# Weight decoding in a Performer and MLP kernel: a third raw buffer, and two pieces of w1 decoded later

## The chip, the cores and the metric

The kernel runs on one core of one Trainium2 chip. The metric is device time in microseconds (us) of one execution, and the figure compared is the median of several executions. The engines are named as the profile names them: PE is TensorE's matmul, PEld its weight load, DVE VectorE, ACT ScalarE, POOL GpSimd and SP SyncE, which issues the DMAs. Each engine takes its own instructions in the order of its queue. The DMAs of this kernel stand nearly all in SyncE's queue, one behind the other.

## The reference

Everything is computed from 64-bit inputs; the kernel reads their words and decodes the weights to 32-bit floats by itself.

```python
def phi(x):                       # random features, omega is 128 x 64
    h = x @ omega.T - sum(x * x) / 2
    return exp(h - max(h)) / sqrt(m)
q_p, k_p = phi(q * scale), phi(k * scale)      # batch 8, heads 8, seq 576, head_dim 64
num = q_p @ (k_p.T @ v)
den = q_p @ sum(k_p)
x = num / (den + 1e-6)                         # heads side by side: 8 x 576 x 512
u = x + (x.T @ U @ V).T                        # mixing along the sequence, rank 32
out = u + relu(u @ w_ch1) @ w_ch2              # w_ch1 512 x 2048, w_ch2 2048 x 512
```

## The kernel before

**Stages.** The first stage is attention: 16 units (pairs of heads), in rounds of nine steps, one step for each tile of 128 positions. A round works on the keys of one unit and the queries of another. In one step TensorE multiplies by the features (`project`, L525 to L527, tile `p_p`), VectorE takes the maximum (L533), ScalarE the exponential (`exp`, L540, tile `e`), and TensorE uses `e` for the keys' sums (L437) or transposes it for the queries (L463). In between runs the mixing along the sequence (`mixing`), which writes rows of `u` to DRAM. The second stage is the MLP over 36 tiles of 128 tokens, in nine chunks: the first of six tiles, seven of four, the last of two.

**The MLP.** The first chunk (`whole_pass`) goes over 16 blocks `f` of 128 hidden features. A block consists of the first product for block f + 1 (`whole1`, L845, 24 matmuls into `p_p`: a group of 512 tokens and one of 256), a relu on ScalarE (L853) and VectorE (L854) for each group, and the second product of block f (`second`, L917, 18 matmuls). All float32 operands are split in a high and a low part, and each product has three passes. The chunks of four tiles take the first product with seven products in place of eight (`products`, L893), pair of blocks by pair of blocks, eight pairs `p` to a chunk; their weight operands `wx` are made once and then read back from DRAM, seven loads a pair (L760).

**Decoding.** `decoding` (L103) is a generator over 35 jobs: one for U, two for V, 16 pieces of w1 (512 columns of 128 rows each) and 16 tiles of w2. A job's 64-bit words come into a tile `raw`, of which there are RB = 2. Then ScalarE takes the magnitude (`mag`, L120), VectorE works on it in a fixed order, one instruction at each step of the generator, and GpSimd adds the low word's share (L164). An early job has five VectorE steps (L139, L140, L143, L146, L147). A late one (number `lean` and up) has three, and a second ScalarE pass makes its low word's share (`low`, L123). The last VectorE step is the last reading of `raw`; behind it the generator asks for the load of job i + RB (L158). The add and what follows are put off into the next job's steps: for w1 a ScalarE copy into `w1f` (L185), for w2 a ScalarE copy into the high part (L177) and a subtraction on GpSimd for the low part (L178). The tiles `mag` and the tag `de` have two buffers each.

**What sets the order.** The code is written in the order in which the work is wanted, and `keep_in_program_order` fixes the order of marked instructions on their engine: the loads of raw weights, VectorE's decoding steps, ScalarE's copies of decoded weights, and nearly all of the MLP. The rest, L120, L123, L164 and L178 among it, is ordered when the program is built, by a simulated timeline. In attention `advance` (L260) takes a decoding step in two of three steps, until `left` = 6 + 5 * EARLY = 66 are used; EARLY = 12 jobs, U, V, six pieces of w1, two tiles of w2 and one piece more. In the MLP's first chunk `each(f, i)` (L997) is called four times a block and takes 1, 2, 1 and 2 decoding steps. From there on, pieces of w1 and tiles of w2 alternate (L198). Block f uses w1's columns for block f + 2 (`Halves`) and w2's tile f.

**Chunks to come.** `Chunk.fetch` (L779) loads a quarter of the next chunk's `u` into a tile `uraw`, of which the pool `up` has three buffers, and `turn` (L784) transposes it on VectorE into `uT`. In the first chunk the fetches come in blocks 6, 7, 8 and 10 and the turns in blocks 9 to 12; in a middle chunk three fetches come at pairs 0, 1 and 2 and the fourth behind the first turn, in pair 5.

Of the kernel before, what the change touches and what calls it, by code (L numbers as in the profile page):

```python
# [9 lines left out]
F32 = mybir.dt.float32  # L10
# [4 lines left out]
ALU = mybir.AluOpType  # L15
# [14 lines left out]
def performer_mlp_kernel(ctx: ExitStack, tc, q, k, v, omega, U, V, w1, w2, out):  # L30
# [7 lines left out]
    nc = tc.nc  # L38
# [3 lines left out]
    DM, DF = w1.shape  # L42
    P = 128
# [7 lines left out]
    NC = DM // P  # L51
    NF = DF // P
# [5 lines left out]
    def f32(ap):  # L58
        return ap.bitcast(F32)

    def words(ap):
        return ap.bitcast(U32)
# [6 lines left out]
    CT, TOK = 4, 4 * P  # L69
# [9 lines left out]
    AHEAD = 2  # L79
    LEAD = AHEAD  # L80
    w1f = const.tile([P, NC, DF], F32, name="w1f")
    w2s = {f: [const.tile([P, DM], F32R, name=f"w2{a}{f}") for a in "hl"] for f in range(AHEAD)}
# [15 lines left out]


    PIECE = 512  # L100
    RB = 2

    def decoding(jobs, late, lean):  # L103

# [7 lines left out]
        def fetch(i):  # L112
            if i < len(jobs):
                raws[i] = dec.tile([P, PIECE, 2], U32, name="raw", bufs=RB)[:, : jobs[i][1], :]
                jobs[i][0](raws[i])
# [8 lines left out]

        for i in range(RB):
            fetch(i)
# [4 lines left out]
        for i, job in enumerate(jobs):  # L131
# [19 lines left out]
            for j, slot in enumerate(slots):  # L151
# [5 lines left out]
                if j == len(slots) - 1:  # L157
                    fetch(i + RB)  # L158
                yield
# [8 lines left out]
            rest.pop(0)()  # L168
            yield

    def weights(src, parts):
        def load(raw):
            tc.keep_in_program_order(nc.sync.dma_start(out=raw.rearrange("p n w -> p (n w)"), in_=words(src)))

        return (
            load, PIECE,
            lambda w: tc.keep_in_program_order(nc.scalar.copy(out=parts()[0], in_=w)),  # L177
            lambda w: nc.gpsimd.tensor_tensor(out=parts()[1], in0=w, in1=f32(parts()[0]), op=ALU.subtract),  # L178
        )

    def w1_job(i):
        f, c = divmod(i, NC)
        fs = slice(f * PIECE, (f + 1) * PIECE)
        load = weights(w1[c * P : (c + 1) * P, fs], None)[0]
        return load, PIECE, lambda w: tc.keep_in_program_order(nc.scalar.copy(out=w1f[:, c, fs], in_=w))  # L185


    N1, FIRST = DF // PIECE * NC, 6

    def w2_job(f):  # L190
        return weights(w2[f * P : (f + 1) * P, :], lambda: w2s[f])

    def weight_jobs():
        for i in range(FIRST):
            yield w1_job(i)
        for f in range(AHEAD):
            yield w2_job(f)
        for i in range(max(N1 - FIRST, NF - AHEAD)):  # L198
            if FIRST + i < N1:
                yield w1_job(FIRST + i)  # L200
            if AHEAD + i < NF:
                yield w2_job(AHEAD + i)

# [54 lines left out]
    def advance(gen, n=1, late=False):  # L260
        for _ in range(n):
            if late or left[0] > 0:
                left[0] -= 1
                if next(gen, gen) is gen:
                    return False
        return True
# [116 lines left out]
    class Part:  # L383
# [20 lines left out]
        def low(self):  # L404
            self.xl.append(wk.tile([P, G * P], F32R, name="xl", bufs=4))
            nc.gpsimd.tensor_tensor(out=self.xl[-1], in0=self.turned, in1=f32(self.xh[-1]), op=ALU.subtract)  # L406
# [196 lines left out]
    }  # L603
    steps = {}
    decoder = decoding([u_job(), *v_jobs(), *weight_jobs()], 6, EARLY)
    mixers = []
    x = None
# [80 lines left out]
    up = ctx.enter_context(tc.tile_pool(name="up", reuse_waits="tile", bufs=2))  # L688
# [82 lines left out]
    class Chunk:  # L771
# [6 lines left out]

        def fetch(self):  # L779
            j = len(self.raws)  # L780
            self.raws[j] = up.tile([P, TOK], F32, name="uraw", bufs=3)[:, : self.n * P]
            fetch(self.c, {j: self.raws[j]})

        def turn(self):  # L784
# [73 lines left out]
        def products(self, w, between):  # L858

            bank = lambda n, b: ps.tile([P, HT], F32, name="p_s", tag=n, bufs=b)  # L860
            X, Y, Z, W = bank("p_p", 2), bank("p_p", 2), bank("p_m", 1), bank("p_kv", 1)
            near = dec.tile([P, 4, HT], F32, name="near", tag="raw", bufs=RB)
            far = dec.tile([P, 2, HT], F32, name="far", tag="de", bufs=2)
# [72 lines left out]
    def take(steps, n=None):  # L936
        while n is None or n > 0:
            if next(steps, steps) is steps:
                return
            n = None if n is None else n - 1  # L940
# [32 lines left out]
    rp = ctx.enter_context(tc.tile_pool(name="rp", side="right", reuse_waits="tile", bufs=2))  # L973
# [21 lines left out]
    pairs, nxt = Weights(0), Chunk(1)  # L995

    def each(f, i):  # L997
        advance(decoder, 1 + i % 2, True)
        if i == 0 and f in (6, 7, 8, 10):
            nxt.fetch()  # L1000
        if 9 <= f < 13 and i == 0:
            nxt.turn()
        if f == 13 and i == 0:
            nxt.prepare()
        if 13 <= f < 15 and i == 1:
            nxt.add()
        if f == 14:
            pairs.add()
            one.residual((4, 5, 0, 1)[i])
        if f == NF - 1:  # L1010
            while advance(decoder, 1, True):
                pass
            while len(pairs.ops) < 5:
                pairs.add()
            while len(nxt.ops) < 3:
                nxt.add()

    steps = whole_pass(one, g, each)
    for c in range(1, NCH - 1):
        now, nxt = nxt, Chunk(c + 1)  # L1020
        short = nxt.n < CT
        for p in range(NH):
            new = None
            if p + 1 < NH or not short:
                new = Weights(p + 1) if c == 1 and p + 1 < NH else Again((p + 1) % NH)
            if p < 3:
                nxt.fetch()
            if p == NH - 1:
                if not short:
                    nxt.add()  # L1030

            def between(i):
                take(steps, 4 - i % 2)
                if p == 6 and i == 6 and not short:
                    nxt.prepare()
                if p > 4 and i % 4 == 0 and nxt.turned < NC:
                    nxt.turn()
                    if nxt.turned == 1:
                        nxt.fetch()
                if len(now.ops) < 7:  # L1040
                    now.add()
                if len(pairs.ops) < 7:
                    pairs.add()
                if new and len(pairs.ops) == 7:
                    new.add()
                    if i == 6:
                        while len(new.ops) < 7:
                            new.add()
                if p == NH - 1 and i < 6:
                    if not short:  # L1050
                        nxt.add()
                    elif i in (0, 2):
                        nxt.short(nxt.uT[:, i : i + 2, :HT], nc.vector)
                    elif i in (1, 3):
                        ws[i // 2] = Halves(i // 2)

            g = now.products(pairs, between)
            take(steps)
            pairs = new
            if p == NH - 1:  # L1060
                for t in range(CT):
                    now.residual(t)
            steps = now.second([p, p + NH], [[x] for x in g], p == 0, p == NH - 1)
# [39 lines left out]
```

## Time and profile before

| | us |
|---|---|
| median of 3 executions | 1155.08 (1154.62 to 1155.59) |
| profiled execution, its own time | 1160.14 |
| its span, first to last instruction | 1158.4 |
| mean granted TensorE clock | 0.975 |

| stage (us of the span) | length | PE busy | DVE busy | ACT busy | POOL busy |
|---|---|---|---|---|---|
| 100 to 200, attention | 100 | 93.27 | 91.46 | 78.23 | 55.44 |
| 200 to 300, attention | 100 | 96.27 | 86.31 | 82.68 | 54.18 |
| 300 to 400, its end and the MLP's begin | 100 | 92.02 | 69.65 | 56.18 | 37.82 |
| 525 to 600, the first middle chunk | 75 | 73.40 | 47.58 | 29.50 | 35.67 |
| 600 to 1095, the other middle chunks | 495 | 495.00 | 233.24 | 111.83 | 26.55 |

A row of a view of waits names who waited, for whom, the time in all, how often and the longest single wait. A row of the chain of waits has a start, a length and what the end of the kernel hung on in that time. A row of the timeline has start, length, engine, line, operation, tiles and count. A row of instruction groups has line, engine, operation, tiles, shapes and count, then busy time and mean ns of one, then the engine's idle time before them. A matmul's end is modelled, so that TensorE's pace is best read from starts.

### The profile page before, as it was taken

To read this page: it belongs to the slowest core of one execution; us is meant where nothing else is said; L and a number is where in the kernel's file an instruction comes from. 1 tells how busy PE (TensorE), PEld (TensorE's weight loads), DVE (VectorE), ACT (ScalarE), POOL (GpSimd) and SP (SyncE) were. 2 spreads that over 40 slices of the span, in tenths; PEclk is the share of its full clock that TensorE was granted. 3 is DMA by queue.
4 is the path that set the end of the run, shared out by engine and by line. 5 is a ranking of instruction groups with operands and counts; after the bars stand their busy time and mean duration, and the time that the engine had idled before them with its cause. 6 is when DMAs were issued, how large, how long until landed. Compare 5 with 4: busy or idle time off the path is not lost.

```text
span 1158.4 us, 20643 instructions
## 1 busy us (share of the span) xinstructions
PE 1107.9 (96%) x7105; PEld 995.1 (86%) x7105; DVE 676.6 (58%) x1475; ACT 500.7 (43%) x1403; POOL 342.6 (30%) x353
## 2 busy tenths in 40 slices
PE   8988989989988989989999999999999999999998
PEld 7988978989967867778988988988999998898887
DVE  4777989977994555455573463463463553553421
ACT  5877868879864554334331132131231221221222
POOL 3435636636315555555420010010100100100133
PEclk9988989999997999989999999999999999999999
DMA  7687676675252345067578687687687687686510
GB/s 130 132 155 137 119 171 135 128 165 103 85 101 82 109 128 128 19 201 236 191 217 232 182 229 220 182 228 220 182 234 212 183 254 193 183 249 187 170 56 19
DMA packets 344360, 187.93 MB, mean 162 GB/s; under 512 B 275872, under 2 KB 275872, under 8 KB 344256
## 3 DMA queue, kind: packets, MB, share of 16 engines
q1 hardware_dynamic: 344192, 186.55, 61.5%
q8 instruction: 57, 0.93, 0.3%
q14 instruction: 47, 0.39, 0.1%
q0 software_dynamic: 64, 0.07, 0.0%
HBM read 152.99 MB, written 33.55 MB: 161 GB/s over the span
## 4 chain that ended last, share of the span: by engine, by line
PE 67%; DVE 8%; DMA 5%; issue 2%; ACT 2%; POOL 1%; SPq 0%; DVEq 0%; ACTq 0%; POOLq 0%
PE p_s L893 23%; PE p_n L917 15%; PE p_q L917 14%; DMA raw<-in_moe_w_ch_dram 4%; PE p_p L845 4%; PE p_n L483 2%; PE p_kv L437 2%; DVE mag L140 2%; PE p_q L463 1%; PE p_p L525 1%; DVE mag L143 1%; PE p_p L526 1%; PE p_p L527 1%; PE py L322 1%; DVE nm L533 1%
## 5 line engine op out<-in xcount | busy, mean ns | idle before, releaser
L893 PEld LDWEIGHTS p_s<-ux,wx 128*128 128x128 f32 x2352 | 336.5, 191 | 43.4 <-ACT near L871 2.6
L893 PE MATMUL p_s<-ux,wx 128*128 128x256 f32 x2352 | 347.2, 284 | 6.1 <-DVE far L701 2.8
L917 PE MATMUL p_n<-w2h,g 128*128 128x512 f32 x576 | 196.6, 398 | 0.0
L917 PE MATMUL p_q<-w2h,g 128*128 128x512 f32 x512 | 191.3, 397 | 0.0
L540 ACT ACTIVATE e<-p_p,nm 128x128 f32<-128x128 f32 x576 | 167.1, 384 | 30.9 <-DVE nm L533 22.1
L406 POOL TENSOR_TENSOR xl<-xT,xh 128x384 fp32r<-128x384 f32 x96 | 100.9, 1067 | 145.4 <-ACT xh L402 107.5
L917 PEld LDWEIGHTS p_n<-w2h,g 128*128 128x128 f32 x576 | 110.0, 191 | 14.4
L814 POOL TENSOR_TENSOR us<-uT 128x512 f32<-128x512 f32 x14 | 19.2, 1368 | 341.1 <-DVE uT L787 341.1
L853 ACT ACTIVATE g<-far 128x256 fp32r<-128x256 f32 x112 | 46.8, 418 | 161.7 <-DVE far L701 161.7
L917 PE MATMUL p_n<-w2l,g 128*128 128x512 f32 x288 | 114.9, 399 | 0.0
L533 DVE TENSOR_REDUCE nm<-p_p 128x4 f32<-128x512 f32 x144 | 97.9, 680 | 28.2 <-PE p_p L527 18.9
L701 DVE TENSOR_TENSOR near<-p_s,near 128x256 f32<-128x256 f32 x168 | 70.4, 419 | 73.7 <-PE p_s L893 71.9
L845 PE MATMUL p_p<-ux,wx 128*128 128x256 f32 (+1 forms) x576 | 100.8, 331 | 11.8 <-DVE g L854 9.7
L845 PEld LDWEIGHTS p_p<-ux,wx 128*128 128x128 f32 x576 | 89.0, 196 | 26.4 <-DVE g L854 12.6
L698 POOL TENSOR_TENSOR wx<-w1f,wx 128x256 fp32r<-128x256 f32 x88 | 66.4, 771 | 129.1 <-ACT wx L697 129.1
L854 DVE SCALAR_TENSOR_TENSOR g<-p_s,g 128x256 fp32r<-128x256 f32 x56 | 23.8, 424 | 135.3 <-ACT g L853 135.3
L917 PEld LDWEIGHTS p_q<-w2h,g 128*128 128x128 f32 x512 | 93.4, 190 | 10.3
L917 PE MATMUL p_q<-w2l,g 128*128 128x512 f32 x256 | 101.5, 397 | 0.0
L853 ACT ACTIVATE g<-p_s 128x256 fp32r<-128x256 f32 x56 | 21.6, 385 | 184.8 <-PE p_s L893 184.6
L525 PE MATMUL p_p<-omh,xh 128*128 128x256 f32 x288 | 95.3, 331 | 0.6 <-ACT e L540 0.3
L854 DVE SCALAR_TENSOR_TENSOR g<-p_p,g 128x256 fp32r<-128x256 f32 (+1 forms) x48 | 24.5, 511 | 110.5 <-ACT g L853 110.5
L526 PE MATMUL p_p<-oml,xh 128*128 128x256 f32 x288 | 83.4, 290 | 0.0
(120 smaller groups left out, 1934.7 us busy)
## 6 DMA issues: line engine op xcount, KB each, us to landing
wx<-wx_dram SPq DMA_DIRECT2D x336, 256.0 KB, 3.0
raw<-in_moe_w_ch_dram SPq DMA_DIRECT2D x32, 512.0 KB, 4.1
wx_dram<-wx SPq DMA_DIRECT2D x56, 256.0 KB, 2.5
u_dram<-ut SPq DMA_DIRECT2D x36, 256.0 KB, 2.1
u<-u_dram SPq DMA_DIRECT2D x36, 256.0 KB, 4.4
out_dram<-u SPq DMA_DIRECT2D x36, 256.0 KB, 3.2
kt<-in_k_dram SPq DMA_DIRECT2D x120, 72.0 KB, 2.8
qt<-in_q_dram SPq DMA_DIRECT2D x120, 72.0 KB, 2.8
```

Of the source, the lines that this page charges most:

```text
L406: nc.gpsimd.tensor_tensor(out=self.xl[-1], in0=self.turned, in1=f32(self.xh[-1]), op=ALU.subtract)
L525: nc.tensor.matmul(o, part.xh[g][:, ts], oh, start=True, stop=False)
L526: nc.tensor.matmul(o, part.xh[g][:, ts], ol, start=False, stop=False)
L533: nc.vector.tensor_reduce(out=self.nm[:, :n], in_=self.pp[:, :n], axis=AX.X, op=ALU.max, negate=True)
L540: nc.scalar.activation(out=self.e[:, j, :], in_=self.pp[:, j, :], func=AF.Exp, bias=self.nm[:, j : j + 1])
L698: keep(rest.tensor_tensor(out=hl[:, 1], in0=x, in1=f32(hl[:, 0]), op=SUBTRACT))
L701: keep(nc.vector.tensor_tensor(out=out, in0=a, in1=b, op=op))
L845: nc.tensor.matmul(ph, l, r, start=(cc + i == 0), stop=(cc == NC - 1 and i == 2))
L853: keep(nc.scalar.activation(out=g[:, 0, ts], in_=x, func=AF.Relu))
L854: keep(nc.vector.scalar_tensor_tensor(out=g[:, 1, ts], in0=x, scalar=0.0, in1=f32(g[:, 0, ts]), op0=ALU.max, op1=ALU.subtract))
L893: tc.keep_in_program_order(nc.tensor.matmul(o, l, r, start=(i in (0, 1, 2, 5) and k + j == 0), stop=(k == 1 and j == 2), skip_group_check= ...
L917: tc.keep_in_program_order(nc.tensor.matmul(po, l, r, start=(begin and n + i == 0), stop=(end and n == len(fs) - 1 and i == 2)))
```

## The change

- RB, the number of `raw` buffers, goes from 2 to 3. The tile `near` of the seven products has the same tag and so three buffers too.
- The subtraction that makes w2's low parts stays on GpSimd for the first two tiles and goes to VectorE for the other 14. It is not marked to keep its place.
- FIRST, the pieces of w1 decoded early, goes from 6 to 4. With it EARLY becomes 10, the early steps 56, and the late jobs 25 of three steps. The late order begins with four pieces of w1 and one tile of w2 (the first of the pieces still as the last early job) and alternates from there.
- In the MLP's first chunk a block takes 2, 2, 2 and 1 decoding steps, seven in place of six.
- `uraw` moves from `up`, three buffers, to the pool `rp`, two buffers. In the first chunk the fetches come in blocks 6, 7, 9 and 10, and behind the turn of the same block; in a middle chunk two come at pairs 0 and 1 and the others behind the first and the second turn.

```diff
-    RB = 2
+    RB = 3
...
-    def weights(src, parts):
+    def weights(src, parts, low=nc.gpsimd.tensor_tensor):
...
-            lambda w: nc.gpsimd.tensor_tensor(out=parts()[1], in0=w, in1=f32(parts()[0]), op=ALU.subtract),
+            lambda w: low(out=parts()[1], in0=w, in1=f32(parts()[0]), op=ALU.subtract),
...
-    N1, FIRST = DF // PIECE * NC, 6
+    N1, FIRST = DF // PIECE * NC, 4
...
     def w2_job(f):
-        return weights(w2[f * P : (f + 1) * P, :], lambda: w2s[f])
+        low = nc.gpsimd if f < AHEAD else nc.vector
+        return weights(w2[f * P : (f + 1) * P, :], lambda: w2s[f], low.tensor_tensor)
...
-        for i in range(max(N1 - FIRST, NF - AHEAD)):
-            if FIRST + i < N1:
-                yield w1_job(FIRST + i)
-            if AHEAD + i < NF:
-                yield w2_job(AHEAD + i)
+        for i in range(FIRST, FIRST + 4):
+            yield w1_job(i)
+        yield w2_job(AHEAD)
+        for i in range(max(N1 - FIRST - 4, NF - AHEAD - 1)):
+            if FIRST + 4 + i < N1:
+                yield w1_job(FIRST + 4 + i)
+            if AHEAD + 1 + i < NF:
+                yield w2_job(AHEAD + 1 + i)
...
-            self.raws[j] = up.tile([P, TOK], F32, name="uraw", bufs=3)[:, : self.n * P]
+            self.raws[j] = rp.tile([P, TOK], F32, name="uraw", bufs=2)[:, : self.n * P]
...
     def each(f, i):
-        advance(decoder, 1 + i % 2, True)
-        if i == 0 and f in (6, 7, 8, 10):
-            nxt.fetch()
+        advance(decoder, 1 + (i < 3), True)
         if 9 <= f < 13 and i == 0:
             nxt.turn()
+        if i == 0 and f in (6, 7, 9, 10):
+            nxt.fetch()
...
-            if p < 3:
+            if p < 2:
                 nxt.fetch()
...
                     nxt.turn()
-                    if nxt.turned == 1:
+                    if nxt.turned < 3:
                         nxt.fetch()
```

## The prediction

> **What bounds the kernel now.** I read the page first, then the waits by engine, the chain of waits, and windows over the two stages that the change touches.
>
> ```profile
> span 1158.4 us, 20643 instructions
> ...
> PE 1107.9 (96%) x7105; PEld 995.1 (86%) x7105; DVE 676.6 (58%) x1475; ACT 500.7 (43%) x1403; POOL 342.6 (30%) x353
> ```
>
> TensorE bounds the whole, so only TensorE's gaps are worth anything. They lie in two stages: attention (up to about 350 us) and the first block of the MLP, which decodes the rest of the weights while it multiplies (about 365 to 475 us). For that second stage the waits are:
>
> ```profile
> POOL mag L164 <- DVE mag L143: 47.4, 23, 4.0
> ...
> ACT low L123 <- DMA raw<-in_moe_w_ch_dram: 25.8, 20, 2.4
> ACT w2h L177 <- POOL mag L164: 22.2, 11, 2.5
> PEld p_p L845 <- DVE g L854: 12.6, 8, 3.9
> PE p_p L845 <- DVE g L854: 9.7, 4, 3.5
> ```
>
> ScalarE waited 25.8 us, in 20 places, for the raw weights to land. It takes its instructions in order, so the relu (L853) behind L123 waited too, then VectorE's half of the relu (L854), and TensorE waited for that one. The chain of waits shows one turn of the loop, two pieces long:
>
> ```profile
> 388.33 4.16 DMA raw<-in_moe_w_ch_dram
> ...
> 392.51 0.02 ACT low L123
> ...
> 393.09 0.59 ACT g L853
> ...
> 393.70 0.69 DVE g L854
> ...
> 394.97 0.43 DVE mag L140
> ...
> 396.49 1.41 DVE mag L140
> ...
> 397.92 0.70 DVE mag L143
> ...
> 398.68 4.74 DMA raw<-in_moe_w_ch_dram
> ```
>
> L143 is a late piece's last reading of its raw buffer. With two buffers the load for the piece after the next can start only then, and its 4.2 to 4.7 us stand in the loop. A turn is 398.68 - 388.33 = 10.35 us and decodes two pieces. What it costs TensorE, from the windows of the first product (L845) and from the chain behind the last piece:
>
> ```profile
> 369.00:482.50 113.50, 54.50 (x289) 46.49 (x290) 0.98 0.39 105
> ...
> 482.62 4.17 PE p_p L845 x24
> ...
> 490.99 1.16 PE p_p L845 x5
> ```
>
> A block has 24 such products. 289 of them are 12 blocks in 113.5 us, 9.46 us each. Without decoding a block takes 490.99 - 482.62 = 8.37 us. The excess is 113.5 - 12 x 8.37 = **13.1 us**.
>
> In attention the same wait is rarer and longer:
>
> ```profile
> ACT mag L120 <- DMA raw<-in_moe_w_ch_dram: 11.5, 5, 3.8
> ...
> ACT low L123 <- DMA raw<-in_moe_w_ch_dram: 3.5, 1, 3.5
> ...
> PE p_q L463 <- ACT e L540: 12.4, 5, 3.7
> ```
>
> Its price I read from the length of rounds of nine steps. Here are the windows between the first L533 of each round (length; L533's busy time and count; granted clock; DMA share; GB/s):
>
> ```profile
> 65.80:88.70 22.90, 6.13 (x9) 0.85 0.84 157
> 88.70:113.00 24.30, 6.12 (x9) 0.86 0.75 148
> ...
> 133.30:158.00 24.70, 6.07 (x10) 0.88 0.66 148
> 158.00:177.70 19.70, 6.02 (x9) 0.98 0.73 161
> 177.70:198.00 20.30, 6.14 (x9) 1.00 0.70 140
> 198.00:218.90 20.90, 6.18 (x10) 1.00 0.59 122
> 218.90:241.00 22.10, 6.00 (x9) 0.99 0.69 154
> 241.00:258.90 17.90, 6.16 (x10) 0.91 0.69 152
> 258.90:276.60 17.70, 6.17 (x9) 1.00 0.66 122
> ```
>
> Three kinds are seen: rounds that decode without a long wait (19.7, 20.3, 20.9: mean 20.3), rounds with one (22.9, 24.3, 24.7, 22.1), and rounds after the last early piece (17.9, 17.7: mean 17.8).
>
> **The change, part by part.**
>
> *Third raw buffer, attention.* Each load now waits for the piece three before it, not two, so it is issued a whole piece earlier: five steps at two in three steps of attention, 7.5 steps or some 17 us at 20.3/9 us a step. Against that the longest wait was 3.8 us. No load should be late any more. The four rounds give back (22.9 + 24.3 + 24.7 + 22.1) - 4 x 20.3 = **12.8 us**. The waits on ScalarE, 15.0 us, bound it from above. From below I take 8, if the last round, which mixes two kinds, and one more give nothing.
>
> The granted clock of 0.85, 0.86 and 0.88 in those rounds is part of their length. The Trainium skill's "TensorE: Matmul & The Clock Gate" (What's actually happening) says that the array drops to half rate after an idle window of about 3.4 us and comes back after as long a busy one. The trace agrees: only the rounds with a wait are that low. By that rule one would add 0.15 x 22.9 + 0.14 x 24.3 + 0.12 x 24.7 = 9.8 us to the gain, as an estimate. I don't, because rounds are compared whole and the clock is in them already.
>
> *Third raw buffer, at the start.* The second piece of V is now loaded at once, not after the first job. Its four transfers stand in SyncE's queue ahead of the third set of values, for which TensorE already waits. The wait, and the same four transfers of the first piece:
>
> ```profile
> PE p_kv L437 <- DMA x<-in_v_dram: 1.7, 1, 1.7
> ...
> 29.09 1.89 SPq L236 DMA_DIRECT2D raw<-in_moe_V_dram  x4
> ```
>
> That costs **1.9 us** if nothing covers it; between 0 and 4, if the gap lowers the clock too.
>
> *Two pieces fewer in attention.* The early steps fall from 66 to 56. A round has six steps, and decoding costs a round 20.3 - 17.8 = 2.5 us, 0.42 us a step; ten steps are **4.2 us**. Between 2 (if the later rounds were shorter for another reason) and 6.
>
> *The same pieces in the MLP, and seven steps a block.* 25 late pieces of three steps take 75 steps, 10.7 blocks of seven; before, 23 pieces took 69, 11.5 blocks of six. A block so decodes 2.33 pieces, not 2. Each has two ScalarE passes over the raw tile (L120, L123) and one copy, three VectorE steps, a GpSimd add, and on SyncE one load of 512 KB that now waits for an older buffer. Cover is TensorE's 8.37 us a block:
>
> ```profile
> 365.00:475.00 110.00, 100.21 (x488) 82.51 (x487) 61.54 (x95) 56.36 (x111) 60.77 (x58) 0.99 0.41 111
> ...
> L178 POOL TENSOR_TENSOR w2l<-mag,w2h 128x512 fp32r<-128x512 f32 x16 | 21.1, 1317 | 4.1 <-ACT w2h L177 4.0
> ...
> L283 DVE TENSOR_TENSOR ml<-x,mh 128x512 fp32r<-128x512 f32 x9 | 6.8, 756 | 0.3 <-ACT mh L282 0.3
> ...
> L140 DVE TENSOR_SCALAR mag<-mag x23: 406/427/1402, 365.8 to 473.6; 128x512 uint32<-128x512 uint32 x23
> ```
>
> These are the block's stage (length, then busy time of PE, PEld, DVE, ACT and POOL), a low part on GpSimd, the same form on VectorE, and one decoding step (shortest, median and longest ns). Busy time for each 9.46 us block is 5.29 us on VectorE, 4.85 on ScalarE, 5.23 on GpSimd. Times 7/6 that is at most 6.2, 5.7 and 6.1.
>
> *Low parts of w2 on VectorE.* 1.17 of them a block leave GpSimd at 1.32 us each (6.1 becomes 4.6) and come to VectorE, where the same form (L283) takes 0.76: 6.2 + 0.9 = 7.1 us, still under 8.37. If the two engines meet it is dearer. L140 takes 0.43 alone and up to 1.40 beside GpSimd's add, 0.98 more; with that on every low part VectorE has 8.2 us a block, barely covered. The Trainium skill speaks against this edit: "Perfetto Trace Analysis" (Optimizing Scalar/DVE Operations) says that the two engines share an SBUF port, so that moving work between them might not help. L140's spread agrees. I count nothing for this move, so the sum is the same by the page.
>
> *What is late next in the block.* The load leaves the loop, since the piece it serves is two pieces, 7 us, further on, against 4.2 to 4.7 us of landing. Left in order are ScalarE's waits for GpSimd's add (22.2 us in 11), which have other work to fill them now, and a shorter lead: the first late w2 piece has its low part at step 15 and is multiplied after step 18; before it was step 6 against 15. I leave 3 us of the 13.1 for these: gain **10 us**, between 7 and 13.1.
>
> *Raw tiles of u in two buffers.* In each of six middle chunks SyncE now waits for a second transposition, with the next pair's weight loads queued behind:
>
> ```profile
> SPq L350 <- DVE uT L787: 17.8, 6, 3.0
> ...
> uraw<-u_dram SPq DMA_DIRECT2D x112, 64.0 KB, 3.9
> ...
> 655.49 0.70 DVE L787 STREAM_TRANSPOSE uT<-uraw 128x512 f32<-128x512 f32 x1
> ...
> 666.13 0.70 DVE L787 STREAM_TRANSPOSE uT<-uraw 128x512 f32<-128x512 f32 x1
> ```
>
> One such wait is 3.0 us. The tile loaded after the second turn (655.49) is transposed at 666.13, 9.9 us after its buffer is free; four issues (1.9 us for V's) and a landing (3.9) are 5.8 us. A weight load has about one pair of lead (10.6 us between the same turns of two pairs). Nothing is counted. The other order of fetch and turn in the first block, the larger decoding pool and its third `near` tile move no work.
>
> **Sum:** 12.8 - 1.9 + 4.2 + 10 = 25.1 us off. The profiled execution took 1160.14 us (span 1158.4), 5.1 above the median of 1155.08, and by the same sum would take 1135.0. The median becomes 1155.1 - 25.1 = **1130.0 us**.
>
> **The rivals.**
>
> *A: the block keeps its pace.* ScalarE's wait for GpSimd's add, already 22.2 us, takes the place of the wait for the load. Then 10 us are lost and the time is 1140. For it: both waits stand on the same in-order engine. Against: 25.8 us of the other go, and ScalarE has 5.7 us of work in 8.37. Chance 0.14.
>
> *B: attention keeps its late loads*, since SyncE reaches them late behind the query and key loads; the third buffer does not do there what it says. 12.8 us are lost: 1142.8. Against: a piece of lead is 17 us. Chance 0.07.
>
> *C, slower: VectorE becomes the bound in the block.* A low part waits in VectorE's order for ScalarE's high part, which waits for GpSimd's add. By the rows that is 2.0 us (22.2/11) and a copy of 0.6; with 0.76 and 0.98 it is 4.4 us for each piece, 5.1 a block. VectorE would have 6.2 + 5.1 = 11.3 us a block: eleven blocks of 11.3 and one of 8.37 are 132.7 us, 19.2 more than now. Against 15.1 from attention the time is 1159. It decides from 10.8 us a block, where a low part holds VectorE 3.9 us. Against: the next piece's steps can stand ahead of it. Chance 0.04.
>
> *D: SyncE's new wait delays the weight loads* of the middle chunks. From 7 us of wait on, each us costs six; 4 us over would eat the gain: 1154, no change. Against: 3.0 us. Chance 0.03.
>
> **How the numbers follow.** The forecast has 0.72. Its own range is the sum of the bounds: 8 - 4 + 2 + 7 = 13 at the least, 15 - 0 + 6 + 13.1 = 34 at the most; the low ends will hardly all meet, so I take 18 to 34, 1121 to 1137. To leave out no more than two in ten it takes in A and B: 1121 to 1143. What a measurement here can tell is 0.2%, 2.3 us. Faster are the forecast, A and B: 0.93; the same is D: 0.03; slower is C: 0.04.
>
> **What would show it.** Right: no wait of L120 or L123 for the raw load over 1 us; rounds of decoding attention near 20.3 us with the clock near 1.0, and the last early decoding step some 40 us sooner; blocks near 8.6 us between 365 and 475; the wait at the third values near 3.6 us. Wrong: blocks still over 9 us, with L177 behind L164 or VectorE's low part behind L177; or new waits at L893 in the middle chunks.

## The result and the profile after

The median after is 1128.73 us (1126.68 to 1130.28, four executions), against 1155.34 us before (1154.62 to 1157.26, four executions). The ratio is 0.9766, with an interval of 0.9745 to 0.9787: 26.6 us off, where 25.1 were forecast. The profiled execution took 1129.66 us of its own (before: 1160.14), with a mean granted clock of 0.983.

First the page's span and busy times, as they were shown of before:

```profile
span 1127.9 us, 20592 instructions
...
PE 1096.9 (97%) x7105; PEld 986.4 (87%) x7105; DVE 683.9 (61%) x1485; ACT 500.2 (44%) x1405; POOL 328.1 (29%) x339
```

TensorE has the same 7105 matmuls, and GpSimd has 14 instructions fewer, the low parts that went to VectorE. Lines behind the weights' part have moved by 5: L845 is now L850, L853 and L854 are L858 and L859, L893 is L898, L533 is L538, L350 is L355, L787 is L792. L120 to L178 stay.

To see where the time went, three stages are cut at two places that each kernel has: the start of the first matmul of the first product (L850 after, L845 before) and the start of the first one of the seven products (L898, L893). The places are the first starts in the views of those two lines, here after (shortest, median and longest ns, first and last start in us):

```profile
L850 PE MATMUL p_p<-ux,wx x576: 274/284/793, 328.8 to 1121.1; 128*128 128x256 f32 x128, 128*128 128x512 f32 x64
L898 PE MATMUL p_s<-ux,wx x2352: 274/283/580, 468.7 to 1072.2; 128*128 128x256 f32 x196
```

| kernel | attention and its end | blocks | rest | median | ratio to before, 95% interval |
|---|---|---|---|---|---|
| before | 350.6 | 148.7 | 659.2 | 1155.34 | |
| before_again, one execution | 351.9 | 144.4 | 658.7 | 1156.73 | |
| after | 328.8 | 139.9 | 659.2 | 1128.73 | 0.9766 (0.9745 to 0.9787) |
| after_again, one execution | 331.0 | 139.4 | 658.3 | 1130.54 | |
| two_buffers | 338.3 | 152.4 | 660.3 | 1151.61 | 0.9974 (0.9946 to 1.0001) |
| buffer_room | 335.8 | 135.8 | 658.3 | 1132.08 | 0.9783 (0.9734 to 0.9832) |
| pieces_only | 337.2 | 155.4 | 658.5 | 1156.18 | 1.0003 (0.9975 to 1.0031) |
| low_on_pool | 329.1 | 142.7 | 658.8 | 1132.12 | 0.9789 (0.9732 to 0.9847) |
| room_only | 350.6 | 146.1 | 661.1 | 1153.93 | 0.9996 (0.9974 to 1.0018) |
| late_fetch | 329.2 | 138.1 | 658.6 | 1127.67 | 0.9769 (0.9741 to 0.9796) |
| v_later | 330.3 | 137.0 | 660.4 | 1128.19 | 0.9767 (0.9730 to 0.9804) |
| five_pieces | 330.9 | 136.1 | 658.1 | 1125.70 | 0.9730 (0.9711 to 0.9748) |
| low_kept | 330.0 | 136.7 | 658.7 | 1124.76 | 0.9726 (0.9707 to 0.9746) |
| five_kept | 329.2 | 136.2 | 659.7 | 1126.09 | 0.9744 (0.9717 to 0.9771) |

The stages are of the one profiled execution, the medians of all. Between the two profiled executions of before the blocks differ by 4.3 us, though it is the same program, and attention by 1.3; a difference of that size in one row of the table proves nothing. Attention gave 21.7 us (20.9 between the second looks), the blocks 8.8 (4.9), the rest nothing.

**Attention after.** The windows between the first L538 of each round, from round 3 to round 10, here with all engines (length; busy time and count of PE, PEld, DVE, ACT and POOL; granted clock; DMA share; GB/s):

```profile
68.10:85.30 17.20, 16.50 (x145) 15.82 (x144) 16.84 (x43) 14.79 (x51) 9.65 (x9) 1.00 0.84 153
85.30:103.90 18.60, 18.20 (x155) 17.33 (x155) 18.23 (x46) 17.11 (x55) 12.40 (x11) 1.00 0.86 149
103.90:124.00 20.10, 20.01 (x164) 19.05 (x163) 19.25 (x44) 19.38 (x61) 15.58 (x14) 1.00 0.85 158
124.00:143.50 19.50, 18.45 (x147) 16.74 (x147) 19.42 (x48) 15.14 (x51) 8.06 (x7) 1.00 0.86 175
143.50:164.10 20.60, 19.36 (x155) 17.60 (x155) 19.58 (x47) 15.29 (x51) 9.26 (x8) 1.00 0.86 196
164.10:183.50 19.40, 18.16 (x147) 16.80 (x147) 19.22 (x45) 17.07 (x53) 14.53 (x12) 1.00 0.72 143
183.50:203.60 20.10, 20.10 (x165) 19.23 (x165) 15.85 (x40) 18.05 (x57) 13.52 (x13) 1.00 0.54 104
203.60:221.10 17.50, 17.50 (x153) 17.11 (x151) 16.52 (x42) 13.90 (x48) 5.91 (x6) 1.00 0.71 160
```

Rounds 3, 4, 6 and 10, which took 22.9, 24.3, 24.7 and 22.1, take 17.2, 18.6, 19.5 and 17.5. The clock is 1.00 in all eight. Before, rounds 3, 4 and 6 each held one stretch at half the clock, as narrower windows over that trace show (length, PE busy and count, granted clock, DMA share, GB/s):

```profile
70.00:76.90 6.90, 6.08 (x28) 0.51 0.73 117
97.30:104.20 6.90, 6.79 (x32) 0.51 0.84 136
152.00:158.80 6.80, 6.53 (x29) 0.50 0.53 135
```

At half the clock these 20.6 us cost 10.3. In ScalarE's waits from 60 to 245 us there is no raw tile any more; the longest row is the maximum of VectorE:

```profile
ACT e L545 <- DVE nm L538: 14.4, 23, 1.6
```

The last decoding step of the early kind (L147) starts at 180.3, before at 228.5, from the view of that line:

```profile
L147 DVE SCALAR_TENSOR_TENSOR de<-raw,de x10: 446/684/1439, 40.2 to 180.3; 128x512 f32<-128x512 uint32 x7, 128x288 f32<-128x288 uint32 x2, 128x320 f32<-128x320 uint32 x1
```

So the round from 183.5, 20.1 us long, has no decoding step at all and is still longer than those from 68.1 and 85.3, which have six each. It has 165 matmuls against their 145 and 155, and TensorE is busy in all of it. In the decoding rounds from 124.0 and 164.1 it is VectorE that is full, with 19.42 us of 19.5 and 19.22 of 19.4.

**The blocks after.** Windows of the first product: nine blocks, then two.

```profile
347.30:422.80 75.50, 39.15 (x217) 34.46 (x217) 1.00 0.53 148
422.80:443.50 20.70, 10.38 (x48) 8.68 (x48) 0.92 0.28 59
```

Nine blocks run at 75.5 / 9 = 8.39 us, TensorE's own pace of 8.37, and so does the one behind the two (8.39). What is left of the loss is in the two blocks from 422.8, 20.7 us in place of 16.8. The waits from 343 to 434 us, to be held against those of the same stage before:

```profile
ACT w1f L185 <- POOL mag L164: 14.7, 9, 2.6
ACT w2h L177 <- POOL mag L164: 14.0, 10, 2.6
...
PE p_p L850 <- DVE g L859: 2.1, 1, 2.1
ACT low L123 <- DMA raw<-in_moe_w_ch_dram: 1.9, 1, 1.9
```

25.8 us of waits for raw weights, in 20 places, have become 1.9 in one. The waits for GpSimd's add did not fall: L177's is 14.0 where it was 22.2, but L185 now waits 14.7 beside it, a row that is not among the waits before. TensorE's one wait for the relu is the long block; its chain:

```profile
423.52 0.72 DVE uT L792
...
424.25 0.33 SPq L355
...
426.28 5.13 DMA raw<-in_moe_w_ch_dram
...
431.50 0.66 ACT low L123
432.16 0.50 ACT g L858
...
432.68 0.70 DVE g L859
...
433.42 0.80 PE p_p L850 x2
```

This is the old chain once more, for the last raw load alone. SyncE waits for a turn (L792) to issue a fetch of `uraw` (L355), the load of the last piece stands behind it, and the relu stands behind L123. At the other end, SyncE's new wait in the middle chunks (560 to 1065 us), and all of TensorE's in the same stretch:

```profile
SPq L355 <- DVE near L706: 25.3, 6, 4.5
```

```profile
PE p_s L898 <- DVE far L706: 0.6, 1, 0.6
```

It stands beside the old wait for `uT` (17.8 us in 6, as before). It is longer than the one it was sized by, and TensorE waits 0.6 us in all.

### The profile page after: what moved, and what is told of

Its sections match the earlier page's. It is cut to its first block, busy times and chain, and to the rows that moved or that the text cites. A ratio compares the mean times of both kernels' runs of the same rounds, so it can differ in the third digit from the quotient of the medians.

```text
span 1127.9 us, 20592 instructions
## 1 busy us (share of the span) xinstructions
PE 1096.9 (97%) x7105; PEld 986.4 (87%) x7105; DVE 683.9 (61%) x1485; ACT 500.2 (44%) x1405; POOL 328.1 (29%) x339
## 4 chain that ended last, share of the span: by engine, by line
PE 73%; DVE 7%; issue 5%; POOL 5%; ACT 4%; DMA 3%; SPq 2%; POOLq 0%; DVEq 0%; ACTq 0%
PE p_s L898 21%; PE p_n L922 15%; PE p_q L922 13%; PE p_p L850 5%; PE p_n L488 4%; PE p_kv L442 3%; POOL wx L703 3%; PE p_p L530 3%; PE p_p L532 2%; PE p_q L468 2%; PE p_p L531 2%; PE py L327 1%; POOL mag L164 1%; DVE mag L143 1%; DVE mag L140 1%
## 5 line engine op out<-in xcount | busy, mean ns | idle before, releaser
L898 PEld LDWEIGHTS p_s<-ux,wx 128*128 128x128 f32 x2352 | 335.6, 190 | 44.0 <-DVE far L706 3.7
L898 PE MATMUL p_s<-ux,wx 128*128 128x256 f32 x2352 | 346.3, 284 | 6.9 <-DVE far L706 4.1
L858 ACT ACTIVATE g<-far 128x256 fp32r<-128x256 f32 x112 | 46.8, 418 | 161.8 <-DVE far L706 161.8
L538 DVE TENSOR_REDUCE nm<-p_p 128x4 f32<-128x512 f32 x144 | 98.0, 681 | 24.7 <-PE p_p L532 16.9
L859 DVE SCALAR_TENSOR_TENSOR g<-p_s,g 128x256 fp32r<-128x256 f32 x56 | 23.8, 425 | 136.2 <-ACT g L858 136.2
L858 ACT ACTIVATE g<-p_s 128x256 fp32r<-128x256 f32 x56 | 21.5, 385 | 187.2 <-PE p_s L898 187.0
L850 PEld LDWEIGHTS p_p<-ux,wx 128*128 128x128 f32 x576 | 89.6, 197 | 16.9 <-POOL wx L703 2.6
L850 PE MATMUL p_p<-ux,wx 128*128 128x256 f32 (+1 forms) x576 | 100.2, 330 | 4.0 <-DVE g L859 2.1
L922 PEld LDWEIGHTS p_q<-w2h,g 128*128 128x128 f32 x512 | 93.7, 191 | 10.3
L859 DVE SCALAR_TENSOR_TENSOR g<-far,g 128x256 fp32r<-128x256 f32 x112 | 49.8, 445 | 54.2 <-ACT g L858 54.2
```

The lines of the kernel that those rows point to most:

```text
L538: nc.vector.tensor_reduce(out=self.nm[:, :n], in_=self.pp[:, :n], axis=AX.X, op=ALU.max, negate=True)
L850: nc.tensor.matmul(ph, l, r, start=(cc + i == 0), stop=(cc == NC - 1 and i == 2))
L858: keep(nc.scalar.activation(out=g[:, 0, ts], in_=x, func=AF.Relu))
L859: keep(nc.vector.scalar_tensor_tensor(out=g[:, 1, ts], in0=x, scalar=0.0, in1=f32(g[:, 0, ts]), op0=ALU.max, op1=ALU.subtract))
L898: tc.keep_in_program_order(nc.tensor.matmul(o, l, r, start=(i in (0, 1, 2, 5) and k + j == 0), stop=(k == 1 and j == 2), skip_group_check= ...
L922: tc.keep_in_program_order(nc.tensor.matmul(po, l, r, start=(begin and n + i == 0), stop=(end and n == len(fs) - 1 and i == 2)))
```

## The experiments

The theory after the result: the third buffer is worth most of it, in both stages; the two pieces fewer in attention give some microseconds there and cost some in the blocks; VectorE's low parts give back what these cost. The rivals: the pieces' order does it without the buffer, or the low parts' move is worth nothing, as the prediction had it.

### The third buffer undone

```diff
-    RB = 3
+    RB = 2
```

> The changed kernel with two raw buffers again, all else as changed. Theory (the third buffer carries the gain): the waits of ScalarE for raw loads return in both stages. Attention loses 10 to 20 us of its 21.7 us of gain; a block of the MLP, which decodes 2.33 pieces at 5.2 us of loop each, takes 10 to 12 us in place of 8.4. In all 1150 to 1170 us. Rival (fewer early pieces, seven steps and VectorE's low parts carry it): at most 1140 us, blocks near 8.6 us.

1151.61 us, 22.9 above after: attention 9.5 longer, the blocks 12.6. ScalarE's waits from 60 to 240 us, the first row, are back; then the waits from 345 to 460:

```profile
ACT mag L120 <- DMA raw<-in_moe_w_ch_dram: 7.4, 4, 3.0
```

```profile
ACT mag L120 <- DMA raw<-in_moe_w_ch_dram: 18.6, 10, 4.0
...
ACT low L123 <- DMA raw<-in_moe_w_ch_dram: 11.6, 9, 2.0
...
PE p_p L850 <- DVE g L859: 9.0, 6, 3.5
```

In attention, rounds 3 and 6 are 23.1 and 23.5 us again, but round 4 stays at 18.7 and round 10, which decodes no more, at 17.9. So two of the four rounds are cured by the pieces and their steps, without a third buffer. The ten blocks from the fourth on take 8.8 to 12.1 us, 10.1 on average, where 10 to 12 were expected.

### The third buffer and the room for it, alone

Before, with `RB = 3`, `uraw` in `rp` with two buffers, and the new order of fetch and turn. The third buffer without the move of `uraw` was not tried.

```diff
-    RB = 2
+    RB = 3
...
-            self.raws[j] = up.tile([P, TOK], F32, name="uraw", bufs=3)[:, : self.n * P]
+            self.raws[j] = rp.tile([P, TOK], F32, name="uraw", bufs=2)[:, : self.n * P]
```

> The kernel before with the third raw buffer, and the raw tiles of u moved to two buffers, without which the third does not fit; six early pieces, six steps and GpSimd's low parts stay. Theory: 20 of the 21.7 us in attention come but for some 4 us of decoding, and 8 to 10 us in the blocks: 1129 to 1135 us, no wait for raw loads over 1 us. Rival (the pieces and steps carry it): over 1145 us.

1132.08 us: alone it gives nearly the whole, 24.3 us (before, measured beside it: 1156.33). Attention is 14.7 shorter. The blocks take 135.8, less than after; they are 12.9 and 8.5 shorter than in the two profiles of before. Rounds 3, 4 and 6 are 17.3, 18.6 and 19.5 us, as after; round 10 stays at 21.7, since it still decodes. Against what was expected, waits for raw loads of up to 1.5 us remain in the blocks. The waits from 345 to 460 us:

```profile
ACT w2h L177 <- POOL mag L164: 30.8, 12, 4.5
...
ACT low L123 <- DMA raw<-in_moe_w_ch_dram: 5.8, 6, 1.5
...
PE p_p L845 <- DVE g L854: 0.4, 1, 0.4
```

ScalarE waits longer for GpSimd's add than before (22.2), and TensorE loses 0.4 us. The wait of the prediction's rival A does arise; the work around it covers it.

### The room alone

Before, with `uraw`'s move and the order of fetch and turn, and two raw buffers.

> The kernel before with the raw tiles of u in two buffers and their fetches moved, and nothing else. Theory: no change, 1152 to 1158 us, the middle chunks' stage at 659 us. Rival (the new waits in SyncE's queue hold up weight loads): each us of delay costs six, 1160 us or more.

1153.93 us, ratio 0.9996 (0.9974 to 1.0018). SyncE's new wait from 600 to 1095 us is there in full, and TensorE has no wait at all in that stretch:

```profile
SPq L350 <- DVE near L701: 25.9, 6, 4.4
```

The rest of this profile is 661.1 us, 2 more than expected; no wait of TensorE in that stretch explains it.

### The kernel before, a second look

> The kernel before once more, for a second profile of its first rounds. Theory (the start's clock varies from one execution to the next): rounds 0 and 1 between 36.7 and 38.6 us, with TensorE's first half-rate time longer than 3.4 us if near the upper end. Rival (the change made the start slower): 36.7 us again.

1156.73 us, with 351.9 us of attention and 144.4 of blocks. It says how far one profile goes: the blocks' term of the prediction was read from an execution whose blocks took 4.3 us more than this one's. The first two rounds take 36.2 us, under the range expected, and the first three 53.4, as in the first look (53.5). That speaks for the rival: two looks at before don't show a start like the one after.

### The pieces and steps alone

Before, with `FIRST = 4`, the late order that begins with four pieces of w1, and seven steps a block; two raw buffers, all low parts on GpSimd.

```diff
-    N1, FIRST = DF // PIECE * NC, 6
+    N1, FIRST = DF // PIECE * NC, 4
...
-        advance(decoder, 1 + i % 2, True)
+        advance(decoder, 1 + (i < 3), True)
```

> The kernel before with four early pieces, the new late order and seven steps a block; two raw buffers and GpSimd's low parts. Theory: attention gains 4 to 8 us, the blocks lose as much or more, since the load stays in the loop and 25 pieces have to pass it: 1150 to 1162 us. Rival: 1145 us or less.

1156.18 us, ratio 1.0003 (0.9975 to 1.0031). It isn't that nothing happens: attention is 13.4 us shorter and the blocks are 6.7 longer in its profile, which took 1152.89, below its median. Ten executions lie between 1152.89 and 1159.93. The waits from 345 to 460 us:

```profile
ACT mag L120 <- DMA raw<-in_moe_w_ch_dram: 14.1, 8, 2.3
...
ACT low L123 <- DMA raw<-in_moe_w_ch_dram: 11.4, 10, 1.8
...
PEld p_p L849 <- DVE g L858: 6.4, 3, 3.3
```

The loads come too late there as before, and more of them are wanted in a block. The whole is as expected, attention's 13.4 is far above the 4 to 8. These 13.4 us and the third buffer's 14.7 together make only 21.5 in low_on_pool: the long round 4 is in both (18.6 us in either), while 3 and 6 need the buffer and 10 needs the pieces (17.4 here, 21.7 in buffer_room).

### All but the low parts' move

```diff
-        low = nc.gpsimd if f < AHEAD else nc.vector
-        return weights(w2[f * P : (f + 1) * P, :], lambda: w2s[f], low.tensor_tensor)
+        return weights(w2[f * P : (f + 1) * P, :], lambda: w2s[f])
```

> The changed kernel with all low parts of w2 on GpSimd. Theory: no engine is the bound in the blocks, so 1128 to 1131 us, the same within what a measurement tells, and blocks at 8.4 us. Rival (GpSimd and its port with VectorE would be late with 2.33 pieces a block): 1133 us or more, blocks over 8.8 us with waits for L178.

1132.12 us, between theory and rival, and the same as buffer_room's 1132.08. Over the third buffer, then, the pieces give 6.7 us in attention (335.8 to 329.1) and take 6.9 in the blocks (135.8 to 142.7), in one profile of each. What of this is the pieces', their order's or the seventh step's was not taken apart. TensorE's waits from 345 to 460 us:

```profile
PE p_p L849 <- DVE g L858: 3.6, 3, 1.6
PE p_n L921 <- POOL w2l L178: 1.2, 3, 0.5
```

TensorE here waits for the low parts themselves, which come late three times. With the low parts on VectorE that row is gone, the wait for the relu is 2.1 us in the first look at after, and in the stage table the blocks take 139.9 and 139.4 in two looks. The median moves from 1132.12 to 1128.73. Against before, measured beside each, that is a gain of 24.2 and of 26.6 us, and the intervals of the two ratios overlap, so that this difference is likely and not shown. The forms side by side, GpSimd in low_on_pool, then VectorE after:

```profile
L178 POOL TENSOR_TENSOR w2l<-mag,w2h x16: 1272/1291/1745, 151.7 to 444.7; 128x512 fp32r<-128x512 f32 x16
```

```profile
L178 DVE TENSOR_TENSOR w2l<-mag,w2h x14: 649/686/694, 357.7 to 440.7; 128x512 fp32r<-128x512 f32 x14
```

### V's third load later

After, with the late fetches of the next experiment, and only two of the three first raw loads at the start; the third, V's second piece, behind the first yields.

```diff
-        for i in range(RB):
+        for i in range(2):
...
+        for i in range(2, RB):
+            fetch(i)
```

> late_fetch, with the load of V's second piece asked for six steps later than the first two loads. Theory (the first two rounds are longer by the clock alone): no change against late_fetch within 3 us, rounds 0 and 1 together 37 to 39 us. Rival (the four transfers at the start cost 1.9 us, as predicted): 2 us faster, the first two rounds at 36.7 us.

1128.19 us, against 1127.67 without this edit: no difference. The first two rounds take 36.9 us, just under the theory's range and near the rival's 36.7, but the third takes 18.2 in place of 17.0. The first three take 55.0 us together, as in two_buffers (55.0), where V's second piece is not loaded at the start either; after takes 55.6, and before 53.5. So the start did become longer without that load too. That the load has no share is not shown: buffer_room, which has it and neither the new pieces nor VectorE's low parts, takes 55.6, and the two looks at after differ by 2.2.

### The last fetches behind the block's loads

After, with the fetches in blocks 9 and 10 at the block's last call in place of its first, so that the last raw load stands ahead of a fetch that waits.

```diff
-        if i == 0 and f in (6, 7, 9, 10):
+        if (i, f) in ((0, 6), (0, 7), (3, 9), (3, 10)):
```

> The changed kernel, with the two fetches of blocks 9 and 10 asked for at the block's last decoding call, not its first, so that they stand behind the last load of raw weights in SyncE's queue. Theory (the last raw load, issued at 426.28 us, was late because it stood behind a fetch that waited for a transposition): the long blocks, 10.64 and 10.09 us, become 8.4 to 9; the blocks' stage goes from 139.9 to about 136 us and the time to 1124 to 1126 us. Rival (the last piece is late for the decoding steps themselves): no change, the long blocks stay.

1127.67 us, where more was expected. The chain around the last load:

```profile
426.00 4.76 DMA raw<-in_moe_w_ch_dram
...
430.84 0.67 ACT low L123
431.51 0.49 ACT g L858
```

The fetch is out of the chain, but the load starts at 426.00 where it had started at 426.28. Its buffer comes free only at the end of L143, 425.05 + 0.68 = 425.73 us in the trace of after, so the start of the load had no more than 0.55 us to win. The two long blocks fall from 10.64 and 10.09 us to 9.80 and 9.29, not to 8.4 to 9. That half of the theory fell: what counts is where the landing's reader stands, not the queue ahead of the load.

### L123 in its place, and one early piece more

Two ways to take the relu out from behind the last load. low_kept is late_fetch with ScalarE's second pass marked to keep its place in the order written:

```diff
-                    nc.scalar.activation(out=lows[i], in_=raws[i][:, :, 0], func=AF.Copy, scale=2.0**-29)
+                    tc.keep_in_program_order(nc.scalar.activation(out=lows[i], in_=raws[i][:, :, 0], func=AF.Copy, scale=2.0**-29))
```

> late_fetch with ScalarE's pass over the low words (L123) marked to keep its place. Theory (what is left of the long blocks is the relu queued behind an L123 that waits for the last raw load): the long blocks (9.80, 9.29 us) fall to 8.4 to 9, the blocks' stage to 135 to 137 us, 1124 to 1128 us. Rival (the order by the simulated timeline is the better one elsewhere): other blocks grow past 8.6 us, 1130 us or more.

five_pieces is after with five early pieces of w1 and so one late job fewer (`FIRST = 5`, the late order still beginning with w1's pieces up to the eighth):

> The changed kernel with five early pieces of w1, so 24 late pieces. Theory (what the pieces give in attention they take from the blocks): attention about 332 us (328.8 with four, 335.8 with six), the blocks' stage 136 to 138 us, in all 1126 to 1130 us, the same. Rival (the early pieces are pure cost): attention longer with no gain in the blocks, 1131 us or more.

low_kept took 1124.76 us, with the first of the two long blocks back at 8.39 us and the other at 9.23. TensorE's wait from 345 to 460 us is 0.5 us, and no wait of ScalarE is for a raw tile.

The reason can be read off its chain of waits in the same stretch: the relu goes before the next piece's L123, and that pass now waits for nothing.

```profile
429.66 0.56 ACT low L123
...
430.82 0.51 ACT g L858
...
433.69 0.56 ACT low L123
```

five_pieces took 1125.70: attention as in the second look at after (330.9 and 331.0), the blocks 3.3 us shorter than in that look, and no wait of TensorE from 340 to 460 us. Both medians are some 3 to 4 us below after, and the intervals of their ratios hardly overlap that of after. low_kept is to be held against late_fetch, from which it differs in the mark alone: 0.9726 against 0.9769, and these intervals overlap a little (0.9707 to 0.9746, 0.9741 to 0.9796).

### After again, and both cures together

> The changed kernel once more, for a second profile. Theory: attention 327 to 331 us, the blocks' stage 137 to 141 us with one or two long blocks behind the last raw load; rounds 3, 4 and 6 as in the first profile within 0.5 us.

1130.54 us, with the long block again: TensorE's waits for L859 from 340 to 460 us are 3.4 us in two, the longest 2.7. Rounds 3, 4 and 6 take 17.2, 18.6 and 19.5 us, as in the first look.

five_kept has five early pieces, the late fetches, and L123 kept in its place.

> The changed kernel with five early pieces, the late fetches and L123 kept in place, all three together. Theory (each of them removes the same thing, the long blocks behind the last raw load): no more than either alone, blocks' stage 135 to 137 us, 1123 to 1126 us. Rival (they add up): below 1122 us.

1126.09 us: the two do not add up, as two cures of one wait would not. low_kept, five_pieces and five_kept are not told apart by their intervals; each has a median below both kernels'.

## Why the prediction was right

The sum was 25.1 us and the medians gave 26.6. Step by step the sizes stand less well than the sum. For attention 12.8 - 1.9 + 4.2 = 15.1 us were forecast and the profiles show 21.7 (20.9 in the second looks); for the blocks 10, and they show 8.8 (4.9). The mechanism was right, a load that stands in the loop for want of a buffer; that the sum came so near is luck in part, since two terms were off in opposite ways.

- **What bounds the kernel.** Right. Undoing the third buffer alone brings back the waits for raw weights and 22.9 us. TensorE bounds the whole, but not every round: in two of the rounds that decode VectorE is full (19.42 of 19.5 us), which would make a decoding step taken out there worth time of its own.
- **Third buffer, attention: 12.8.** Mechanism right, size too low: 14.7 alone, with a longer start already taken off. Rounds 3, 4 and 6 gave 5.7 + 5.7 + 5.2 = 16.6 us after, where the base of 20.3 us leaves 11.0 for them. So the mis-sized step is that base, and ScalarE's 15.0 us did not bound these rounds from above. The base came from rounds 7 to 9, but the rounds from 183.5 after and from 68.1 show that rounds differ by 3 us for what else they hold, decoding or not. The trace bears out that the clock is inside the term and not beside it: the three stretches at half the clock cost 10.3 us and are part of the 16.6. To add the 9.8 of the estimate to the term, as the rule of the Trainium skill's "TensorE: Matmul & The Clock Gate" (What's actually happening) could be used, would have made 22.6 and too much.
- **Third buffer, at the start: 1.9 lost.** A loss is there (the first three rounds take 55.6 us after and 57.8 in after_again, against 53.5 and 53.4 before), but not in the way that was told: the wait at the third values, which was to grow to 3.6 us, no longer shows among TensorE's waits from 20 to 60 us. two_buffers and v_later lose 1.5 us without the load; buffer_room loses 2.1 with it and without the pieces. What share the load has stays open.
- **Two pieces fewer in attention: 4.2.** 6.7 over the third buffer, in one profile of each, a little above the upper bound of 6. It is uneven: of the ten steps round 9 held six and takes 20.1 us in low_on_pool in place of 20.9 in buffer_room, round 10 held four and takes 17.9 in place of 21.7. Again the base was a mean over unlike rounds.
- **The blocks: 10.** 8.8 in the profile, 4.9 in the second looks. The loop through the load is gone, as said, and nine blocks are at 8.39 us. The 3 us left over for a shorter lead came out elsewhere: 20.7 - 2 x 8.37 = 4.0 us in two blocks, at the last raw load. The 13.1 to start from were those of one execution; before_again spent 4.3 less in the stage, and 4.9 of gain is below the lower bound of 7.
- **The same pieces and a seventh step in the blocks: held to be covered.** They cost 6.9 us, from 135.8 to 142.7, with all low parts on GpSimd. Buffer and pieces together so give less than the buffer alone, and this is where the blocks' 10 us were too many.
- **Low parts on VectorE: 0.** The blocks are 2.8 and 3.3 us shorter in the two looks at after than in the one at low_on_pool, which is likely a gain and not shown to be one. The two engines do get in each other's way, as the view of the tile `mag` from 340 to 440 us shows:

```profile
L140 DVE TENSOR_SCALAR mag<-mag x25: 417/428/1466, 343.6 to 436.2; 128x512 uint32<-128x512 uint32 x25
```

  Its longest is 1.47 us, its median 0.43. The timeline tells the two kinds apart: the eight that take 1.18 us or more run beside GpSimd's add (L164), the 17 that take 0.43 or less beside nothing of GpSimd. So the rule of the Trainium skill's "Perfetto Trace Analysis" (Optimizing Scalar/DVE Operations), that a move between these two might not help, has its ground here. That the move cost nothing all the same may lie in how soon a low part is ready, 0.69 us against 1.29; this is argued and not shown.
- **`uraw` in two buffers: 0.** Right. The new wait was sized at 3.0 us and came out at 25.3 / 6 = 4.2 on average, 4.5 at most; the 7 us from which it would cost anything were not reached.
- **The rivals.** A: its wait for GpSimd's add arises in buffer_room (30.8 us) and after (14.0 and 14.7), and costs TensorE 0.4 us in buffer_room and nothing that shows after. B: ScalarE has no wait for a raw load in attention. C: VectorE makes the low parts and nine blocks still take 8.39 us each; the length of a block that would have eaten the 15.1 comes out at (113.5 + 15.1 - 8.37) / 11 = 10.9 us by the prediction's own terms, not 10.8. D: room_only shows its wait and no loss.
- **The signs.** Right were the clock at 1.00 in the decoding rounds (which take 17.2 to 20.6 us, not near 20.3 throughout), blocks near 8.6 us (nine of 8.39) and the last early step sooner (48 us, where 40 were said). Not met were the wait at the third values and, once, the 1 us: L123 waits 1.9 us for the last raw load, and the two blocks there take 10.64 and 10.09 us, over the 9 that were to show the prediction wrong. Neither L177 nor VectorE's low part stands in that chain.

## What to carry to other kernels

When an in-order engine waits for a load, look who stands behind that wait: here it was relus that have nothing to do with the load, and one more buffer, or the waiting instruction kept in its written place, let them go. When a gain is read from stretches of a kernel, compare each stretch with one that does the same work otherwise, and take a second profile before a stage of one execution is made the base of a sum. Terms that cure the same wait don't add up (13.4 + 14.7 gave 21.5, and the two cures of the last load gave no more than one).

## What the runs showed of the hardware

TensorE's clock at the start differs between programs, and between two executions of one. Two windows over the start, before and after (length, PE busy and count, granted clock, DMA share, GB/s):

```profile
10.00:20.00 10.00, 8.19 (x48) 0.83 0.73 151
20.00:30.00 10.00, 9.92 (x86) 1.00 0.69 117
```

```profile
10.00:20.00 10.00, 7.90 (x42) 0.71 0.73 151
20.00:30.00 10.00, 10.00 (x58) 0.61 0.69 116
```

TensorE is fully busy from 20 to 30 us after, and yet at 0.61, with 58 matmuls in place of 86. In these 20 us the clock took 2.9 + 3.9 = 6.8 us after, and 1.7 before (1.7 more from 30 to 40 us). In after_again, the same program as after, the second window has 0.92 and the loss comes later, from 50 to 60 us (0.71). Narrower windows, one before and one after, show what the shares are made of:

```profile
15.40:18.80 3.40, 3.40 (x18) 0.50 0.69 144
14.10:27.80 13.70, 13.39 (x63) 0.50 0.74 132
```

The clock is at half there and full beside it. Both looks at before have 6.8 to 6.9 us at half in their first three rounds, in two stretches of about 3.4 (the second look's from 15.3 and 29.0); buffer_room has one of 10.2 from 14.6, after the one of 13.7, after_again two of 6.8 and 6.9 from 14.8 and 48.9. They look like whole numbers of 3.4 us, and each costs 1.7. After, TensorE was busy for 13.39 of 13.7 us and the clock stayed at half, so that a busy time of 3.4 us, as the prediction put it, did not bring it back at once.

The Trainium skill's "TensorE: Matmul & The Clock Gate" (What's actually happening) says that the number of slow matmuls at the start varies from run to run, as the window in which activity is counted runs freely; the two looks at after agree that the place varies, while the time at half is 13.7 us in both. Why after and two_buffers lose more there than both looks at before stays open. It is a likely part of the start's 2 to 4 us, which no experiment here has isolated.
